# The scores of two heads in the two halves of the array's rows, and the mask as further products

## The chip, the cores and the metric

The kernel runs on one core of a Trainium2 chip. The metric is the device time of one execution in microseconds. Three runs of the kernel before gave 319.25, 321.22 and 318.66 us, a median of 319.25 us. The engines are written as in the profile: PE is TensorE's products and PEld its weight loads, DVE is VectorE, ACT is ScalarE, POOL is GpSimd, SP is SyncE.

## What is computed

A block-sparse attention is followed by a feed-forward block with a residual. For each query row an upper bound of its scores is worked out for each chunk of 32 keys from the chunk's least and greatest key values; the six chunks with the largest bounds are kept, and the softmax runs over the kept keys that are not in the future. Inputs are float32, with 4 batches, 8 heads, 768 rows and a head dimension of 64; the feed-forward block has a width of 512 and a hidden width of 2048.

```python
k_min = np.min(k_chunks, axis=3)
k_max = np.max(k_chunks, axis=3)
ub = np.sum(np.maximum(q[:, :, :, None, :] * k_min[:, :, None, :, :], q[:, :, :, None, :] * k_max[:, :, None, :, :]), axis=-1)
ub = np.where(causal, ub, -1000000000.0)
top_chunks = np.argsort(ub, axis=-1)[..., -top_k:]
scores = scale * np.matmul(q, k.transpose(0, 1, 3, 2))
mask = sel & (pos[:, None] >= pos[None, :])
scores = np.where(mask, scores, -1000000000.0)
attn = softmax(scores)
attn_out = np.matmul(attn, v)
...
xn = (x - mu) / np.sqrt(var + 1e-06) * g_ln
ch = np.maximum(xn @ w_ch1, 0.0) @ w_ch2
return x + ch
```

## The kernel before

The 768 rows are 6 tiles of 128 (`NT`), taken in two halves of 3 tiles (`NR`, `TR`). The 32 heads are taken as 16 pairs (`g`, of which `HP` = 4 belong to one batch). A pair's q and k are loaded half by half with the two heads side by side (`load_qk`, L189, on SP's queue) and turned by TensorE, so that rows 0 to 63 of a turned tile hold head 0 and rows 64 to 127 head 1 (`turn`, L210). v comes through POOL's queue (`load_v`, L198), one transfer a head.

Then, for each pair, or for each half of the first four pairs:

- `k_bound` (L252) takes the chunks' minima and maxima on VectorE; `k_diag` (L274) spreads them over a block layout with `hsel`, in the order of the heads that the mask needs.
- `bounds` (L291) works out the upper bounds by products. In the first four pairs it first runs six products on TensorE whose results nobody reads (`IDLE`).
- `select` (L322) finds the sixth largest bound (`max`) and writes a mask `mn` with 1 where a chunk isn't chosen; `mask_t` (L341) turns it on TensorE, and `mask_ring` (L347) copies it from there.
- `scores` (L385) forms the scores of one half of the rows in bins of at most four blocks of 128 by 128 and applies the exponential with ScalarE (L403). The first half has 2 bins, the second 4. `diag` (L408) cuts the diagonal blocks on POOL, `values` (L415) multiplies by v, `normalise` (L428) divides by the sum, `pair_stats` (L453) takes the statistics for the layer norm.

The scores and the mask are one product of 128 rows. For each head there are tiles of four ring places: `KA` and `QA` for head 0, `KB` and `QB` for head 1. In `KA` rows 0 to 63 are head 0's keys and rows 64 to 127 a constant pattern `RT`, which says for each key in which chunk it lies (times a large negative number). In `QA` rows 0 to 63 are the queries and rows 64 to 127 the turned mask. `KB` and `QB` have the halves the other way round. So a product sums the score and the mask's penalty in one pass:

```python
nc.tensor.matmul(
    sc[:, hh, o:o + w * P], ks[:, t * P:(t + 1) * P], qs[:, s * P:(s + w) * P],
    start=True, stop=True,
)
```

The rings are filled in three ways. In the first four pairs ScalarE copies each 64-row half straight from the turned tile (L227, L228, L266, L267). In the other twelve it copies all 128 rows to `qh` and `kh` (L237, L270), and SP moves the halves into the rings by four transfers for the keys (L271, L272, twice) and two for the queries (`q_ring`, L248). VectorE copies the two halves of the mask (L350, L351), sets the constant rows (`ring_rows`, L107) and clears places without a mask (`ring_init`, L103).

For each batch and half, `stats`, `centre` and `x_t` (L479) make the normalised, turned rows, `mlp1` (L491) and `mlp2` (L504) run the feed-forward block, `rstd` (L477, POOL) and L516 finish a tile, and SP stores it (L521). w1 and w2 are loaded through POOL's queue in four transfers each; a small copy from a pair's `kc` ahead of each one holds it back (`w1_load`, L158, and `w2_load`, L163).

The order of work comes from two lists. `begin` is a hand-made order for the first four pairs and the first rows of batch 0, kept on each compute engine by dependencies (the last lines of the function). All else has a due time (`at(t, ...)`) and is issued sorted by it; a pair takes one unit of time, and the feed-forward work of the last batch is spread between the pairs of the next. The feed-forward work of batch 3 comes last.

Of the kernel before, what the change touches and what calls it, by code (L numbers as in the profile page):

```python
# [19 lines left out]
def kernel(  # L20
# [23 lines left out]
    VW = 72  # L44
    HP = H // 2
    NG = B * HP
# [14 lines left out]
    ring = ctx.enter_context(tc.tile_pool(name="ring", bufs=1))  # L61
# [29 lines left out]
    NK = 4  # L91
    QA = [ring.tile([P, S], F16, name=f"QA{i}", tag=f"QA{i}") for i in range(NK)]
    QB = [ring.tile([P, S], F16, name=f"QB{i}", tag=f"QB{i}") for i in range(NK)]
    KA = [ring.tile([P, S], F16, name=f"KA{i}", tag=f"KA{i}") for i in range(NK)]
    KB = [ring.tile([P, S], F16, name=f"KB{i}", tag=f"KB{i}") for i in range(NK)]

    NB = 3
    BD = [ring.tile([P, 2, 2, NCH], F32, name=f"BD{i}", tag=f"BD{i}") for i in range(NB)]
    BH = [ring.tile([P, 2, 2, 2, NCH], F16, name=f"BH{i}", tag=f"BH{i}") for i in range(NB)]
    NM = 3  # L100
    MN = [ring.tile([P, NT - 1, P], F16, name=f"MN{i}", tag=f"MN{i}") for i in range(NM)]

    def ring_init(i):  # L103
        nc.vector.memset(QA[i][64:P, 0:P], 0.0)
        nc.vector.memset(QB[i][0:64, 0:P], 0.0)

    def ring_rows(i):  # L107
        nc.vector.tensor_copy(KA[i][64:P, :], RT[0:64, :])
        nc.vector.tensor_copy(KB[i][0:64, :], RT[0:64, :])

    def consts_first():
# [10 lines left out]
        )  # L122
        nc.gpsimd.memset(causb, 0.0)
# [6 lines left out]
        nc.vector.memset(hsel[0:64, 0, 1:2], -KS)  # L130
        nc.vector.memset(hsel[64:P, 0, 0:1], -KS)
        nc.vector.memset(hsel[0:64, 1:3, 1:2], KS)
        nc.vector.memset(hsel[64:P, 1:3, 0:1], KS)
# [64 lines left out]
    def load_v(g, i=None):  # L198
        b, hp = divmod(g, HP)
        a, z = (0, NT) if i is None else parts(g)[i]  # L200
        if not i:
            st[g]["va"] = vap.tile([P, 2, NT, VW], F16, name="va", tag="va")
            nc.gpsimd.memset(st[g]["va"][:, :, :, D:D + 1], 1.0)
        for hh in range(2):
            nc.gpsimd.dma_start(  # L205
                st[g]["va"][:, hh, a:z, 0:D],
                v[b, 2 * hp + hh, a * P:z * P].rearrange("(t p) d -> p t d", p=P),
            )
# [10 lines left out]
    def q_copy(g, i):  # L219
        pst = st[g]["qn", i]  # L220
        if g < HP:
            u = P if i == 0 else 0
            for e, (nm, sign) in enumerate((("q32", -1.0), ("r32", 1.0))):
                st[g][nm] = prp.tile([P, TR * P], F32, name=nm, tag=nm)
                nc.scalar.activation(st[g][nm][:, u:], pst[:, u:], ACTF.Relu, scale=sign)
            c = cols(g, i)
            nc.scalar.activation(QA[g % NK][0:64, c], pst[0:64, :], ACTF.Copy, scale=QS)  # L227
            nc.scalar.activation(QB[g % NK][64:P, c], pst[64:P, :], ACTF.Copy, scale=QS)  # L228
            return
        if i == 0:  # L230
            for nm in ("q", "r"):
                t2 = prp.tile([P, 2, S], F16, name=nm + "2", tag=nm + "32")
                st[g][nm + "h"], st[g][nm + "l"] = t2[:, 0], t2[:, 1]
        qh, ql = st[g]["qh"], st[g]["ql"]
        a, z = parts(g)[i]
        u = slice(max(a, 1) * P, z * P)
        nc.scalar.activation(qh[:, cols(g, i)], pst, ACTF.Copy, scale=QS)  # L237
# [9 lines left out]

    def q_ring(g):  # L248
        nc.sync.dma_start(QA[g % NK][0:64, :], st[g]["qh"][0:64, :])
        nc.sync.dma_start(QB[g % NK][64:P, :], st[g]["qh"][64:P, :])  # L250

# [133 lines left out]
    def scores(g, r, i):  # L385
# [6 lines left out]
        for hh in range(2):  # L392
            qs = (QA if hh == 0 else QB)[g % NK]
            ks = (KA if hh == 0 else KB)[g % NK]
            o = 0
            for t, s, w in bins[i]:
                nc.tensor.matmul(  # L397
                    sc[:, hh, o:o + w * P], ks[:, t * P:(t + 1) * P], qs[:, s * P:(s + w) * P],
                    start=True, stop=True,
                )  # L400
                o += w * P
# [139 lines left out]
    begin = [(warm, 8)] + [(ring_init, i) for i in range(NK)] + [(ring_rows, 0)]  # L541
# [6 lines left out]
    for n in range(-3, U):  # L548
# [26 lines left out]
        if n < 0:  # L575
            begin += [(ring_rows, n + 4)]
# [17 lines left out]
    for g in range(HP, NG):  # L594
# [13 lines left out]
        at(T - 1.4, q_ring, g)  # L608
# [89 lines left out]
```

## Time and profile before

| what | value |
|---|---|
| median of three runs | 319.25 us |
| profiled execution, its own time | 319.25 us |
| its span, first to last instruction | 317.5 us |
| granted TensorE clock, mean | 0.993 |
| score products, L397 (two lines of the page: 224 each) | 448 products, 34.8 + 34.1 us shown |
| w1 products, L498, and w2 products, L510 | 95.8 us and 96.6 us shown |
| exponential, L403 | 96 instructions, 85.8 us |
| load of v, L205 | 40 issues, 833 ns each on POOL |
| transfers into the rings | KA, KB 24 each of 48 KB; QA, QB 12 each of 96 KB |

A product's length in such a table is from its start to its modelled end, and products overlap, so the sum of lengths is more than the time they take of the engine; the distance from start to start is what one costs. A name like `KA` stands for all its places. The share of an engine is an average over the span, and a stretch of the span can have another bound.

### The profile page before, as it was taken

The page shows a single profiled execution, that of the slowest core. Times are in us where ns is not written, and L with a number is a line of the kernel's source. Part 1 is how long each engine was busy: PE and PEld are TensorE (multiplying, and loading weights), DVE is VectorE, ACT ScalarE, POOL GpSimd, SP SyncE. Part 2 cuts the span into 40 slices and gives each one's busy share as a digit, 9 for nine tenths or more (in the row PEclk, how much of TensorE's full clock was granted, in tenths as well). Part 3 has the DMA queues.
Part 4 walks back from the last instruction along what each step waited for, and adds up shares of the span by engine and source line. Part 5 has one row for each costly group of instructions (what it writes and reads, how often), then busy time and mean ns, then how long its engine had stood idle before and what let it go on. Part 6 is the DMA issues. An engine that isn't in the chain of part 4 may idle for free.

```text
span 317.5 us, 7210 instructions
## 1 busy us (share of the span) xinstructions
PE 293.0 (92%) x2756; PEld 196.3 (62%) x2756; DVE 190.4 (60%) x646; ACT 183.7 (58%) x274; POOL 98.4 (31%) x174
## 2 busy tenths in 40 slices
PE   7868699977999999889999998999999999999994
PEld 4867376654678767566676756766666565555541
DVE  7877734548977688988856677756653453000021
ACT  4998386544497765567857575566555653333210
POOL 9527705139535434533432122212120211000000
PEclk9999799999999999999999999999999999999999
DMA  7989994999957489464964021020200000100011
GB/s 130 210 152 210 206 188 78 196 171 129 219 138 106 106 133 154 138 77 116 148 81 104 35 77 41 12 72 25 62 35 35 33 33 2 66 35 33 33 69 67
DMA packets 90419, 31.42 MB, mean 99 GB/s; under 512 B 78608, under 2 KB 87312, under 8 KB 90384
## 3 DMA queue, kind: packets, MB, share of 16 engines
q1 hardware_dynamic: 60416, 23.61, 31.7%
q0 software_dynamic: 29440, 7.34, 24.3%
q8 instruction: 22, 0.36, 0.5%
q14 instruction: 13, 0.11, 0.1%
q10 hardware_dynamic: 528, 0.00, 0.1%
HBM read 27.27 MB, written 6.29 MB: 106 GB/s over the span
## 4 chain that ended last, share of the span: by engine, by line
PE 65%; DVE 13%; issue 6%; DMA 5%; POOL 4%; ACT 4%; SPq 2%; ACTq 0%; POOLq 0%
PE yp L510 24%; PE mm L498 19%; PE mm L397 7%; PE sm L423 5%; PE tr L214 4%; DMA w2b<-in_moe_w_ch_dram 3%; PE ub L317 3%; DVE bst L457 2%; PE trh L483 2%; POOL va L205 2%; DVE x L433 2%; SPq L194 2%; DVE xc L468 2%; DMA qn<-in_q_dram 1%; ACT pt L403 1%
## 5 line engine op out<-in xcount | busy, mean ns | idle before, releaser
L403 ACT ACTIVATE pt<-mm 128x1024 f16<-128x1024 f32 x96 | 85.8, 917 | 38.8 <-PE mm L397 38.1
L510 PE MATMUL yp<-w2b,hT 128*128 128x512 f16 x384 | 96.6, 379 | 1.9 <-DMA w2b<-in_moe_w_ch_dram 1.9
L498 PE MATMUL mm<-xT,w1b 128*128 128x384 f16 x512 | 95.8, 329 | 1.4 <-ACT pt L403 1.2
L502 ACT ACTIVATE hT<-mm 128x768 f16<-128x768 f32 x64 | 51.9, 811 | 57.0 <-PE mm L498 56.8
L498 PEld LDWEIGHTS <-w1b 128*128 128x128 f16 x512 | 49.4, 99 | 33.5 <-issue 3.6
L410 POOL TENSOR_SCALAR_AFFINE_SELECT pt<-pt 128x768 f16<-128x768 f16 x32 | 29.5, 923 | 96.6 <-ACT pt L403 96.6
L510 PEld LDWEIGHTS <-hT 128*128 128x128 f16 x384 | 36.9, 98 | 34.6 <-DMA w2b<-in_moe_w_ch_dram 2.3
L516 DVE SCALAR_TENSOR_TENSOR ot<-yp,rstd,x 128x512 f32<-128x512 f32 x24 | 17.9, 745 | 55.9 <-PE yp L510 54.0
L397 PE MATMUL mm<-QA,KA 128*128 128x128 f16 (+2 forms) x224 | 34.8, 245 | 1.0 <-ACT hT L502 0.9
L397 PE MATMUL mm<-QB,KB 128*128 128x128 f16 (+2 forms) x224 | 34.1, 246 | 0.1
L205 POOL DMA_DIRECT2D va<-in_v_dram x40 | 33.0, 833 | 1.0 <-issue 0.5
L423 PEld LDWEIGHTS <-pt 128*128 128x128 f16 x672 | 25.4, 98 | 6.2 <-issue 1.1
L423 PE MATMUL sm<-va,pt 128*128 128x65 f16 x672 | 27.0, 193 | 1.2 <-ACT QB L228 1.0
L432 DVE RECIPROCAL rden<-sm 128x6 f32<-128x6 f32 x32 | 6.2, 193 | 31.8 <-PE sm L423 31.8
L397 PEld LDWEIGHTS <-KA 128*128 128x128 f16 x224 | 17.9, 98 | 7.4 <-issue 1.0
L457 DVE BATCH_NORM_STATS2 bst<-x 128x6 f32<-128x128 f32 x96 | 21.7, 280 | 0.8
L397 PEld LDWEIGHTS <-KB 128*128 128x128 f16 x224 | 17.9, 98 | 4.2 <-issue 1.3
L238 DVE SCALAR_TENSOR_TENSOR q<-tr,q 128x256 f16<-128x256 f32 (+1 forms) x24 | 11.6, 485 | 14.5 <-ACT q L237 14.2
L259 DVE TENSOR_REDUCE kc<-tr 128x12 f32<-128x384 f32 x32 | 17.5, 546 | 4.5 <-PE tr L214 4.5
L433 DVE TENSOR_TENSOR x<-sm,rden 128x384 f32<-128x384 f32 x32 | 17.8, 556 | 1.0
L483 PE MATMUL trh<-ident_h,xc 128*128 128x128 f16 x96 | 10.5, 224 | 7.7 <-DVE xc L468 6.5
L214 PE MATMUL tr<-ident_f,qn 128*128 128x128 f32 x96 | 16.2, 278 | 1.5 <-DMA qn<-in_q_dram 1.5
(83 smaller groups left out, 349.9 us busy)
## 6 DMA issues: line engine op xcount, KB each, us to landing
kn<-in_k_dram SPq DMA_DIRECT2D x64, 96.0 KB, 3.0
qn<-in_q_dram SPq DMA_DIRECT2D x64, 96.0 KB, 3.5
out_dram<-ot SPq DMA_DIRECT2D x24, 256.0 KB, 2.1
va<-in_v_dram POOLq DMA_DIRECT2D x24, 96.0 KB, 4.4
w1b<-in_moe_w_ch_dram POOLq DMA_DIRECT2D x4, 512.0 KB, 8.1
w2b<-in_moe_w_ch_dram POOLq DMA_DIRECT2D x4, 512.0 KB, 8.9
KA<-kh SPq DMA_DIRECT2D x24, 48.0 KB, 2.0
KB<-kh SPq DMA_DIRECT2D x24, 48.0 KB, 2.0
```

Of the source, the lines that this page charges most:

```text
L205: nc.gpsimd.dma_start(st[g]["va"][:, hh, a:z, 0:D], v[b, 2 * hp + hh, a * P:z * P].rearrange("(t p) d -> p t d", p=P),)
L214: nc.tensor.transpose(pst[:, t * P:(t + 1) * P], src[:, t], ident_f)
L397: nc.tensor.matmul(sc[:, hh, o:o + w * P], ks[:, t * P:(t + 1) * P], qs[:, s * P:(s + w) * P], start=True, stop=True,)
L403: nc.scalar.activation(pt[:, n0:n1].rearrange("p n h x -> p h n x"), sc[:, :, 0:o].rearrange("p h (n x) -> p h n x", x=P), ACTF.Exp, scale ...
L410: nc.gpsimd.affine_select(out=dv, in_=dv, compare_op=ALU.is_ge, fill=0.0, base=0, pattern=[[0, 2 * TR], [1, P]], channel_multiplier=-1,)
L423: nc.tensor.matmul(pv[:, hh, s2, :], pt[:, where[t, s], hh, :], va[:, hh, t, 0:D + 1], start=(t == 0), stop=(t == s),)
L433: nc.vector.tensor_tensor(xh(b, r)[:, :, 2 * hp:2 * hp + 2, :].rearrange("p s h d -> p h s d"), pv[:, :, :, 0:D], rden.to_broadcast([P, 2, ...
L457: nc.vector.bn_stats(h["st"][:, i, hp], xh(b, r)[:, i, 2 * hp:2 * hp + 2].rearrange("p h d -> p (h d)"),)
L498: nc.tensor.matmul(hp_[:, i, 0:TR * P], w1b[:, kt, (m + i) * P:(m + i + 1) * P], h["xT"][:, kt], start=(kt == 0), stop=(kt == KT1 - 1),)
L502: nc.scalar.activation(h["hT"][:, m:m + 2], hp_[:, :, 0:TR * P], ACTF.Relu, scale=HS)
L510: nc.tensor.matmul(yp, h["hT"][:, kt, i * P:(i + 1) * P], w2b[:, kt, :], start=(kt == 0), stop=(kt == KT2 - 1),)
L516: nc.vector.scalar_tensor_tensor(ot, yp, h["rstd"][:, i:i + 1], xh(b, r)[:, i].rearrange("p h d -> p (h d)"), op0=ALU.mult, op1=ALU.add,)
```

## The change

It lets each head's scores be a product of 64 rows: head 0 from rows 0 to 63 of `kh` and `qh`, head 1 from rows 64 to 127 of the same tiles. The mask is added by further products of 64 rows, of `RT` and the turned mask `mt`, into the same sums. `RT` has its pattern in both halves now. For each bin the products of the scores come first and then those of the mask, and the heads alternate. Block (0,0) needs no mask product. A bin of one head is one sum: its first product starts it, its last one ends it.

The rings with their copies and transfers go (`ring_init`, `ring_rows`, `q_ring`, L271, L272). `qh`, `kh` and `mt` come from a pool with five buffers each; BD, BH and MN move to the constants' pool. In the first four pairs a half's keys or queries are copied by one instruction of 128 rows, and the mask everywhere by one. `hsel` has the heads in their own order. For the pairs from 4 on v is loaded by one transfer a pair. Twelve products whose results nobody reads (`idle`, 128 by 512) come before the first `x_t`.

```diff
+    NK = 5
...
-    ring = ctx.enter_context(tc.tile_pool(name="ring", bufs=1))
+    ring = ctx.enter_context(tc.tile_pool(name="ring", bufs=NK))
...
+        nc.vector.tensor_copy(RT[64:P, :], RT[0:64, :])
...
     def load_v(g, i=None):
         b, hp = divmod(g, HP)
-        a, z = (0, NT) if i is None else parts(g)[i]
+        if i is None:
+            va = st[g]["va"] = vap.tile([P, 2, NT, VW], F16, name="va", tag="va")
+            nc.gpsimd.memset(va[:, :, :, D:D + 1], 1.0)
+            nc.gpsimd.dma_start(
+                va[:, :, :, 0:D].rearrange("p h t d -> p (h t) d"),
+                v[b, 2 * hp:2 * hp + 2].rearrange("h (t p) d -> p (h t) d", p=P),
+            )
+            return
+        a, z = parts(g)[i]
...
-            c = cols(g, i)
-            nc.scalar.activation(QA[g % NK][0:64, c], pst[0:64, :], ACTF.Copy, scale=QS)
-            nc.scalar.activation(QB[g % NK][64:P, c], pst[64:P, :], ACTF.Copy, scale=QS)
+        if i == 0:
+            st[g]["qh"] = ring.tile([P, S], F16, name="qh", tag="qh")
+        qh = st[g]["qh"]
+        nc.scalar.activation(qh[:, cols(g, i)], pst, ACTF.Copy, scale=QS)
+        if g < HP:
             return
...
-    def q_ring(g):
-        nc.sync.dma_start(QA[g % NK][0:64, :], st[g]["qh"][0:64, :])
-        nc.sync.dma_start(QB[g % NK][64:P, :], st[g]["qh"][64:P, :])
...
     def k_copy(g, i):
         pst = st[g]["kn", i]
-        c = cols(g, i)
-        if g < HP:
-            nc.scalar.copy(KA[g % NK][0:64, c], pst[0:64, :])
-            nc.scalar.copy(KB[g % NK][64:P, c], pst[64:P, :])
-            return
-        kh = smp.tile([P, TR * P], F16, name="kh", tag="kh")
-        nc.scalar.copy(kh, pst)
-        nc.sync.dma_start(KA[g % NK][0:64, c], kh[0:64, :])
-        nc.sync.dma_start(KB[g % NK][64:P, c], kh[64:P, :])
+        if i == 0:
+            st[g]["kh"] = ring.tile([P, S], F16, name="kh", tag="kh")
+        nc.scalar.copy(st[g]["kh"][:, cols(g, i)], pst)
...
-        nc.vector.tensor_copy(QA[g % NK][64:P, a * P:z * P], pm[64:P, 0:(z - a) * P])
-        nc.vector.tensor_copy(QB[g % NK][0:64, a * P:z * P], pm[0:64, 0:(z - a) * P])
+        if i is None or i == 0:
+            st[g]["mt"] = ring.tile([P, S], F16, name="mt", tag="mt")
+        nc.vector.tensor_copy(st[g]["mt"][:, a * P:z * P], pm[:, 0:(z - a) * P])
...
+    def idle(n, w=512):
+        junk = ps_t.tile([P, 512], F32, name="idle", tag="one")
+        for _ in range(n):
+            nc.tensor.matmul(junk[:, 0:w], MN[0][:, 0, :], MN[0].rearrange("p s c -> p (s c)")[:, 0:w], start=True, stop=True)
...
         sc = ps_m.tile([P, 2, 512], F32, name="mm", tag="mm")
-        for hh in range(2):
-            qs = (QA if hh == 0 else QB)[g % NK]
-            ks = (KA if hh == 0 else KB)[g % NK]
-            o = 0
-            for t, s, w in bins[i]:
+        o, todo = 0, []
+        for t, s, w in bins[i]:
+            todo.append((st[g]["kh"], st[g]["qh"], t, s, w, o))
+            o += w * P
+        for _, _, t, s, w, f in todo[:]:
+            c = int(s == 0)
+            if w > c:
+                todo.append((RT, st[g]["mt"], t, s + c, w - c, f + c * P))
+        for n, (ks, qs, t, s, w, f) in enumerate(todo):
+            for hh in range(2):
+                row = slice(64 * hh, 64 * hh + 64)
                 nc.tensor.matmul(
-                    sc[:, hh, o:o + w * P], ks[:, t * P:(t + 1) * P], qs[:, s * P:(s + w) * P],
-                    start=True, stop=True,
+                    sc[:, hh, f:f + w * P], ks[row, t * P:(t + 1) * P], qs[row, s * P:(s + w) * P],
+                    start=(n == 0), stop=(n == len(todo) - 1),
                 )
-                o += w * P
...
-    begin = [(warm, 8)] + [(ring_init, i) for i in range(NK)] + [(ring_rows, 0)]
+    begin = [(warm, 8)]
...
-            begin += [(x_t, 0, 0, kt) for kt in range(KT1)]
+            begin += [(idle, 12)] + [(x_t, 0, 0, kt) for kt in range(KT1)]
...
-        if n < 0:
-            begin += [(ring_rows, n + 4)]
...
-        at(T - 1.4, q_ring, g)
```

More of the change, by code (lines that the diff above doesn't have):

```diff
@@ L90 @@
     mhalf = const.tile([P, TR], F32, name="mhalf", tag="mhalf")
[L91 to L95, printed above, removed]
     NB = 3
-    BD = [ring.tile([P, 2, 2, NCH], F32, name=f"BD{i}", tag=f"BD{i}") for i in range(NB)]
-    BH = [ring.tile([P, 2, 2, 2, NCH], F16, name=f"BH{i}", tag=f"BH{i}") for i in range(NB)]
+    BD = [const.tile([P, 2, 2, NCH], F32, name=f"BD{i}", tag=f"BD{i}") for i in range(NB)]
+    BH = [const.tile([P, 2, 2, 2, NCH], F16, name=f"BH{i}", tag=f"BH{i}") for i in range(NB)]
     NM = 3
[L101 to L109, printed above, removed]
+    MN = [const.tile([P, NT - 1, P], F16, name=f"MN{i}", tag=f"MN{i}") for i in range(NM)]
     def consts_first():
@@ L129, in consts_first @@
         nc.scalar.activation(tiny, hsel[0:1, 0, 0:1], ACTF.Exp)
[L130 to L133, printed above, removed]
+        nc.vector.memset(hsel[0:64, 0, 0:1], -KS)
+        nc.vector.memset(hsel[64:P, 0, 1:2], -KS)
+        nc.vector.memset(hsel[0:64, 1:3, 0:1], KS)
+        nc.vector.memset(hsel[64:P, 1:3, 1:2], KS)
         for i in range(NM):
@@ L225, in q_copy @@
                 nc.scalar.activation(st[g][nm][:, u:], pst[:, u:], ACTF.Relu, scale=sign)
-            c = cols(g, i)
-            nc.scalar.activation(QA[g % NK][0:64, c], pst[0:64, :], ACTF.Copy, scale=QS)
-            nc.scalar.activation(QB[g % NK][64:P, c], pst[64:P, :], ACTF.Copy, scale=QS)
+        if i == 0:
[3 more added lines that the diff above has]
+        if g < HP:
             return
         if i == 0:
[L231 to L234, printed above, removed]
+            t3 = prp.tile([P, 3, S], F16, name="q3", tag="q3")
+            st[g]["ql"], st[g]["rh"], st[g]["rl"] = t3[:, 0], t3[:, 1], t3[:, 2]
+        ql = st[g]["ql"]
         a, z = parts(g)[i]
         u = slice(max(a, 1) * P, z * P)
-        nc.scalar.activation(qh[:, cols(g, i)], pst, ACTF.Copy, scale=QS)
         nc.vector.scalar_tensor_tensor(
```

## The prediction

> **What bounds the kernel now.** I read the page's first part and the chain of waits first, to see which engine sets the end.
>
> ```profile
> PE 293.0 (92%) x2756; PEld 196.3 (62%) x2756; DVE 190.4 (60%) x646; ACT 183.7 (58%) x274; POOL 98.4 (31%) x174
> ...
> PE 65%; DVE 13%; issue 6%; DMA 5%; POOL 4%; ACT 4%; SPq 2%; ACTq 0%; POOLq 0%
> ```
>
> TensorE is busy 92% of the span and makes up 65% of the chain. But 92% is an average, so next I asked for the busy time by stages.
>
> ```profile
> 13.00:17.40 4.40, 3.42 (x47) 3.35 (x46) 3.13 (x10) 4.31 (x10) 0.85 (x1) 1.00 1.34 213
> ...
> 36.80:40.20 3.40, 3.40 (x17) 2.11 (x15) 1.36 (x9) 0.53 (x2) 2.49 (x5) 0.57 1.26 190
> 40.20:45.00 4.80, 4.33 (x36) 3.29 (x35) 1.90 (x5) 4.74 (x10) 0.00 (x0) 1.00 1.35 196
> ...
> 75.00:80.00 5.00, 3.08 (x30) 1.89 (x27) 4.51 (x14) 0.87 (x2) 5.00 (x10) 1.00 1.88 165
> ...
> 125.00:137.00 12.00, 10.05 (x112) 6.42 (x112) 11.10 (x33) 7.14 (x11) 6.30 (x10) 1.00 0.65 128
> ...
> 198.00:250.00 52.00, 52.00 (x509) 34.79 (x510) 29.65 (x100) 30.74 (x41) 8.64 (x15) 1.00 0.13 37
> ```
>
> After the stretch and its length the columns are PE, PEld, DVE, ACT, POOL (busy us and count), the granted clock and the DMA share. The reader sees three regimes. In 13 to 17.4 and 40.2 to 45 ScalarE is full (4.31 of 4.40, 4.74 of 4.80). In 75 to 80 and 125 to 137 VectorE is nearly full and TensorE has holes. In 198 to 250 TensorE has none at all. The idle time of TensorE between 40 and 262 us is small, and its waits say whose it is:
>
> ```profile
> PE trh L483 <- DVE xc L468: 4.0, 4, 1.9
> PE yp L510 <- DMA w2b<-in_moe_w_ch_dram: 1.9, 1, 1.9
> PE mm L498 <- ACT pt L403: 1.2, 3, 0.5
> PE mm L397 <- ACT hT L502: 0.9, 2, 0.5
> ```
>
> So from 40 us on any added TensorE time goes almost whole into the end, and relief of the other engines can win only these few microseconds. Last, the price of products, from the timeline of TensorE (start, length, group):
>
> ```profile
> 118.40 1.07 PE L423 MATMUL sm<-va,pt 128*128 128x65 f16 x30
> 119.31 0.39 PE L397 MATMUL mm<-QA,KA 128*128 128x128 f16 x4
> 119.54 0.39 PE L397 MATMUL mm<-QB,KB 128*128 128x128 f16 x4
> 119.76 0.25 PE L317 MATMUL ub<-BH,q 128*128 128x96 f16 x2
> ```
>
> A product is shown 219 ns long, but eight start within 0.45 us: 56 ns per 128 columns. The 30 products of 65 columns start within 0.91 us, 30 ns each, and each of them loads new weights. The loads are hidden.
>
> **The score products.** Per pair and head there are 21 blocks of 128 columns in 14 products, so the kernel has 448 products and 16 x 42 = 672 blocks, at about 55 ns some 37 us. Afterwards each head has the same 14 products with 64 rows, and 13 more with 64 rows that add the mask (20 blocks, as block (0,0) has none): 864 products in 432 twos, one of each head. If the two of a two run at the same time in the two halves of the array, the time is that of 16 x 41 = 656 blocks: 16 x 55 ns = **0.9 us less**. If they run one after the other, 1312 blocks are 640 more than now, +35 us. No row of this trace has two products at once. The narrowest step the trace shows for load and product is 30 ns, so a two needs up to 60 ns where 128 columns need 56. 17 of the 27 twos of a pair are that narrow: 272 x 4 ns = **1.1 us more**, the value I take, because the weight path of the 30 ns row is the nearest thing to what a two asks for; 0 and +35 us stay as ends. By the span model of "TensorE: Matmul & The Clock Gate" (Part 3, packing small matmuls) a further row tile would add about 4 ns: an estimate of 432 x 4 ns = 1.7 us in place of the 1.1 us, which no run here shows.
>
> **The changes of the tile's shape.** All products of before are 128*128. In the instruction order of the changed kernel the 864 form 93 runs between 128-row products: 186 changes. The nearest row is a change of operand type: at 13.48 the last f16 score product (256 columns, 105 ns) is followed at 13.59 by an f32 transpose, with no gap beyond its columns. That bounds a change from below at **0**; a gain is excluded since nothing is removed there. From above it is the whole overlap lost, 219 - 56 = 163 ns, 186 x 163 = 30 us. I take 0 by the nearest row, and keep the upper end. "TensorEngine Tiling (Array Packing)", Key Properties, speaks against the change: it says that switching the tiling mode drains the engine. It names no time; a drain as long as the overlap would make the sum some 30 us worse, the row makes it nothing.
>
> **ScalarE at the front.** In the first eight half-pairs four copies of 64 rows (L227, L228, L266, L267; 473 to 486 ns) become two of 128 rows, and a copy's time follows its columns: 477 to 494 ns for 128x384 at L270 and L237. That is 16 x 0.48 = 7.7 us of ScalarE. What is on the path:
>
> ```profile
> 16.50 0.48 ACT L228 ACTIVATE QB<-tr 64x384 f16<-64x384 f32 x1
> ...
> 17.04 0.52 PE L423 MATMUL sm<-va,pt 128*128 128x65 f16 x12 [0.98 <-ACT QB L228]
> ```
>
> The first values product waits 0.98 us for L228 behind a full ScalarE; with one copy less ahead of it, 0.9 us go. From 17.4 to 31.7 the loop is another: values, L433, the statistics (0.68), maxima, mask transposes, bounds, values again, about 5 us, none of it removed: 0. In 40.2 to 45 ScalarE is full again and TensorE waits for it (0.47 us at L397, as much before L498): 0.9 us.
>
> **The twelve idle products.** They stand before the x_t of the first half, where TensorE now idles 1.89 + 0.43 + 0.16 us and then runs at clock 0.50 from about 36.8 to 39.7. Eight w1 products there take 320 ns each instead of 162: 1.3 us. The idle products (12 x 216 = 2.6 us, the spacing of 512 columns in L510) end at about 35.2, before the third xc at 35.6, which is waited for anyway; they cost 0.1. I take 1.2 us.
>
> These three, **3.0 us**, must pass the w2 transfer that TensorE waits for until 66.7. Its issue stands on POOL behind the diag of 50.56, which waits for an exp at 49.46, so it moves with the front. If the transfers do not come earlier, these 3.0 us are lost: that end is 0.
>
> **VectorE.** The two mask copies of 64 rows (495 and 480 ns) become one of 128: 0.48 us for each of the 12 later pairs, 0.28 for the first ones, and ring_rows and ring_init (4.1 us before 13 us, beside transfers that are waited for) go against one RT copy of about 0.45. It counts only where TensorE waits for VectorE: 75 to 80, 125 to 137, 137 to 147, 184 to 198, four stretches, of which one copy lies before the xc in each: at most 4 x 0.48 = 1.9, I take **1.5 us**; lower end 0.
>
> **Queues.** The 72 transfers from SBUF to SBUF leave SP, where kn and qn loads stood behind the waits of L271 (34.9 us in all). TensorE waits for no load after 11 us, so 0. One copy on ScalarE waited 3.7 us for such a transfer near 76, beside the xc wait of 1.92 that set the pace there: nothing beyond the term above. POOL issues 12 loads of v fewer: 12 x 0.83 us, in stretches where it waits for ScalarE (96.6 us), so 0; if one issue of twelve tiles took twice as long, it would be 0 too. The new ring of five for kh, qh and mt is waited for by none, as the reader of a buffer is five pairs back.
>
> **The sum**, from the profiled run (319.25 us, of which 317.5 is the span, and also the median of the three): -0.9 + 1.1 + 0 - 3.0 - 1.5 = -4.3, so **315.0 us**. It would be no different by more than 1% between 316.1 and 322.4.
>
> **Rivals.**
> - *The change of shape empties the array* (slower). Place: each of about 176 changes behind the front. For it: nothing covers TensorE in 198 to 250. Against it: the change of type is free. At half of its bound, 82 ns, it costs 14 us: **329 us**. It decides from 4.3 us / 186 = 23 ns on, and costs over 1% from about 41 ns (7.4 us). Chance 0.25.
> - *The halves do not run together*: 315 + 35 = **350 us**. PEld of the 128-row products is hidden now, which says nothing of halves. Chance 0.10.
> - *The relief stays off the path*: the w2 transfers land when they do now, and VectorE's copies lie in waits. What is left is -0.9 + 1.1 and the 1.0 us or so of single waits: **318.5 us**. For it: DMA is over 1.2 in most of 36 to 66 us. Chance 0.18; 0.02 more for small changes of shape that just cancel the gain.
> - *More goes*: the waits listed above vanish as well, about 5 us: **310 us**. Chance 0.05.
>
> My own case has 0.40, with a range of its own of 311 to 316. So faster has 0.45, same 0.20, slower 0.35. The range goes from 309 to 333: it leaves out the serial case and the upper end of the first rival, 0.16, and 0.03 below.
>
> **What will show it.** Right: a run of 7 twos (4 of the scores, 3 of the mask, all of 128 columns) passes in about 0.42 us and the next group starts without a gap; the first values product starts near 16.1; the clock is 1.00 in 36 to 40; the wait for w2 ends near 63.7; the stretch of 52 products at the end is unchanged. Wrong: gaps of tens of ns at both ends of each run of 64-row products, or steps of 56 ns for each single one, either of which would show in a longer 198 to 250; or an exposed wait for w2 that has grown by what the front won.

## The result and the profile after

The changed kernel takes 330.64 us, the median of four runs (330.31 to 334.62); the kernel before took 319.91 us beside it (four runs, 318.66 to 321.22). The ratio is 1.036, with an interval of 1.027 to 1.046: 3.6% slower. The profiled execution took 330.31 us, of which 328.1 are its span, against 319.25 and 317.5 before; so the two traces are 11.06 us apart.

First the page of the changed kernel: busy time by engine, the chain of waits by engine and by line, and from the list of the costliest groups the score products, the mask products and the weight loads in front of the former (after the bar: idle time just before them, and what ended most of it). "Issue" is time in which an engine waited for nothing that the profile can name.

```profile
PE 309.9 (94%) x3184; PEld 191.0 (58%) x3184; DVE 177.6 (54%) x611; ACT 177.2 (54%) x258; POOL 90.4 (28%) x162
...
PE 75%; DVE 16%; ACT 3%; SPq 2%; issue 1%; DMA 1%; POOL 1%; POOLq 0%
PE yp L508 24%; PE mm L496 22%; PE mm L396 9%; PE sm L421 5%; PE tr L211 4%; PE ub L304 3%; DVE bst L455 3%; DVE x L431 2%; PE ub L294 2%; PE trh L481 2%; SPq L183 2%; PE trh L332 1%; DVE xc L466 1%; DVE q L235 1%; ACT hT L500 1%
...
L396 PE MATMUL mm<-qh,kh 64*128 64x128 f16 (+2 forms) x448 | 37.0, 246 | 2.4 <-ACT pt L401 1.3
L396 PE MATMUL mm<-mt,RT 64*128 64x128 f16 (+2 forms) x416 | 33.9, 245 | 0.0
...
L396 PEld LDWEIGHTS <-kh 64*128 64x128 f16 x448 | 15.6, 94 | 22.5 <-issue 20.0
```

All that the change was to relieve is relieved: VectorE has 177.6 us instead of 190.4, ScalarE 177.2 instead of 183.7, POOL 90.4 instead of 98.4. DMA has gone from 5% of the chain to 1%. TensorE has gone from 65% to 75%. The last line is the one to stop at. The weight loads stood idle for 20.0 us ahead of the score products with the releaser "issue": they waited for no semaphore, no transfer, no engine that the profile names. The kernel before had 1.0 and 1.3 us of that at the same place, for head 0 and head 1:

```profile
L397 PEld LDWEIGHTS <-KA 128*128 128x128 f16 x224 | 17.9, 98 | 7.4 <-issue 1.0
...
L397 PEld LDWEIGHTS <-KB 128*128 128x128 f16 x224 | 17.9, 98 | 4.2 <-issue 1.3
```

Then the stretches, with the columns of the prediction's table (PE, PEld, DVE, ACT, POOL, clock, DMA share, GB/s). They are fixed in time, so the later ones hold somewhat other work than before.

```profile
13.00:17.40 4.40, 4.40 (x63) 3.90 (x59) 2.92 (x10) 3.66 (x7) 0.85 (x1) 1.00 1.36 205
36.80:40.20 3.40, 3.40 (x33) 2.41 (x31) 1.66 (x5) 3.21 (x7) 2.00 (x3) 1.00 1.44 216
40.20:45.00 4.80, 4.80 (x60) 3.21 (x61) 1.14 (x4) 2.38 (x3) 0.00 (x0) 1.00 1.38 207
75.00:80.00 5.00, 5.00 (x43) 2.64 (x42) 4.90 (x12) 1.53 (x3) 2.81 (x5) 1.00 1.99 182
125.00:137.00 12.00, 9.87 (x119) 5.62 (x116) 10.59 (x33) 6.05 (x9) 5.75 (x10) 1.00 0.49 83
198.00:250.00 52.00, 51.17 (x557) 30.17 (x555) 29.66 (x102) 29.40 (x40) 9.19 (x15) 1.00 0.06 22
```

At the front TensorE is full where it had holes, ScalarE is no longer full, and the clock is 1.00 in 36.8 to 40.2 where it was 0.57. In 198 to 250, where TensorE had no idle time before, it is still shown busy for 51.17 of 52 us. That number hides the loss: a product of 128 columns is shown some 220 ns long whatever its distance from the next, so a gap of 100 ns between starts doesn't appear as idle time of PE. It must be read from the starts. The waits of TensorE for other engines, at least, have shrunk, and the w2 transfer is no longer among them:

```profile
PE trh L481 <- DVE xc L466: 3.6, 5, 1.3
PE trh L332 <- DVE MN L323: 2.9, 4, 1.0
...
PE mm L396 <- ACT pt L401: 1.3, 3, 0.6
```

Now the starts, from the timeline of TensorE (start, length, group) around one bin of a later pair. The bin has one score product and four mask products for each head, 128 columns each:

```profile
206.98 1.03 PE L508 MATMUL yp<-w2b,hT 128*128 128x512 f16 x4
207.94 0.23 PE L396 MATMUL mm<-qh,kh 64*128 64x128 f16 x2
208.01 0.39 PE L396 MATMUL mm<-mt,RT 64*128 64x128 f16 x8
208.32 0.66 PE L496 MATMUL mm<-xT,w1b 128*128 128x384 f16 x3
```

and the weight loads of the same time:

```profile
206.87 0.64 PEld L508 LDWEIGHTS <-hT 128*128 128x128 f16 x4
207.94 0.10 PEld L396 LDWEIGHTS <-kh 64*128 64x128 f16 x2 [0.42 <-issue]
207.95 0.27 PEld L396 LDWEIGHTS <-RT 64*128 64x128 f16 x8
208.32 0.44 PEld L496 LDWEIGHTS <-w1b 128*128 128x128 f16 x4
```

Two things are read here. Ten products of 128 columns pass between 207.94 and 208.32, in 0.38 us; one after the other they would need 10 x 56 ns = 0.56. So the two products of a two (one of each head) do run together: in the trace most start 3 to 4 ns apart (377 of the 421 that can be told apart; 32 start 16 to 20 ns apart), and twos follow each other every 56 ns. And 0.38 is 0.10 more than 5 x 56 ns. The last two starts at 208.18 and the next w1 product, of 128 rows, 148 ns later instead of 56. At the other end the last w2 product starts at 207.63 and the first two 312 ns later, where w2 products of 512 columns are 216 ns apart. The loads show the same gap: none of the new shape starts before 207.94, when the first product of that shape starts too, 0.10 us behind the columns of the last w2 product (0.42 us of "issue").

Over the whole trace a change between f16 products of the two shapes has a median of 98 to 99 ns beyond the columns, in both directions (97 to an f32 transpose); products of one shape have 2 to 3 ns. The second two of a 64-row run starts another 10 ns later than that (median of 74 runs). There are 186 changes: 186 x 97 ns = **18.0 us**. How the difference grows along the run (start of the same product before and after, and the difference less 97 ns for each change up to then):

| product | before | after | difference | less the changes |
|---|---|---|---|---|
| first values product | 17.04 | 15.47 | -1.57 | -1.76 |
| w1, first | 36.86 | 35.31 | -1.55 | |
| w1, ninth | 40.24 | 37.34 | -2.90 | |
| w2, 13th | 66.73 | 63.13 | -3.59 | -6.11 |
| values, 169th | 89.73 | 85.65 | -4.08 | -7.96 |
| w2, 97th | 163.24 | 165.28 | +2.04 | -8.24 |
| w2, 241st (all scores done) | 263.81 | 274.85 | +11.04 | -7.00 |
| w2, last | 312.54 | 323.59 | +11.04 | -7.00 |

The kernel is 4 us ahead at 86 us, loses that and 11 us more by 275 us at the pace of the changes, and nothing after the last bin. By this count the rest has won 7.0 us without the changes. The last column takes the full 97 ns for each change, also where TensorE would have waited anyway, so its rows near the front are too large; the first experiment has the leads without any change.

### The profile page after: what moved, and what is told of

Same layout as the page of the kernel before. It is cut to its first block, busy times and chain, and to the rows that moved or that the text cites. A ratio compares the mean times of both kernels' runs of the same rounds, so it can differ in the third digit from the quotient of the medians.

```text
span 328.1 us, 7854 instructions
## 1 busy us (share of the span) xinstructions
PE 309.9 (94%) x3184; PEld 191.0 (58%) x3184; DVE 177.6 (54%) x611; ACT 177.2 (54%) x258; POOL 90.4 (28%) x162
## 4 chain that ended last, share of the span: by engine, by line
PE 75%; DVE 16%; ACT 3%; SPq 2%; issue 1%; DMA 1%; POOL 1%; POOLq 0%
PE yp L508 24%; PE mm L496 22%; PE mm L396 9%; PE sm L421 5%; PE tr L211 4%; PE ub L304 3%; DVE bst L455 3%; DVE x L431 2%; PE ub L294 2%; PE trh L481 2%; SPq L183 2%; PE trh L332 1%; DVE xc L466 1%; DVE q L235 1%; ACT hT L500 1%
## 5 line engine op out<-in xcount | busy, mean ns | idle before, releaser
L401 ACT ACTIVATE pt<-mm 128x1024 f16<-128x1024 f32 x96 | 86.8, 918 | 48.9 <-PE mm L396 48.5
L496 PE MATMUL mm<-xT,w1b 128*128 128x384 f16 x512 | 94.1, 326 | 0.8 <-ACT pt L401 0.7
L408 POOL TENSOR_SCALAR_AFFINE_SELECT pt<-pt 128x768 f16<-128x768 f16 x32 | 27.7, 865 | 113.1 <-ACT pt L401 113.1
L508 PEld LDWEIGHTS <-hT 128*128 128x128 f16 x384 | 35.2, 98 | 37.3 <-issue 6.1
L396 PE MATMUL mm<-qh,kh 64*128 64x128 f16 (+2 forms) x448 | 37.0, 246 | 2.4 <-ACT pt L401 1.3
L396 PE MATMUL mm<-mt,RT 64*128 64x128 f16 (+2 forms) x416 | 33.9, 245 | 0.0
L396 PEld LDWEIGHTS <-kh 64*128 64x128 f16 x448 | 15.6, 94 | 22.5 <-issue 20.0
L235 DVE SCALAR_TENSOR_TENSOR q<-tr,qh 128x256 f16<-128x256 f32 (+1 forms) x24 | 11.7, 489 | 18.8 <-ACT qh L226 18.6
L259 ACT CAST kh<-tr 128x384 f16<-128x384 f32 x32 | 15.5, 484 | 10.5 <-DVE kc L253 8.9
L252 DVE TENSOR_REDUCE kc<-tr 128x12 f32<-128x384 f32 x32 | 17.6, 549 | 6.5 <-PE tr L211 6.5
L396 PEld LDWEIGHTS <-RT 64*128 64x128 f16 x416 | 17.2, 94 | 2.0
L431 DVE TENSOR_TENSOR x<-sm,rden 128x384 f32<-128x384 f32 x32 | 17.8, 556 | 0.9
L253 DVE TENSOR_REDUCE kc<-tr 128x12 f32<-128x384 f32 x32 | 17.6, 549 | 0.0
```

The source lines that it names most:

```text
L252: nc.vector.tensor_reduce(kc[:, 0, n], view, axis=AX.X, op=ALU.min)
L396: nc.tensor.matmul(sc[:, hh, f:f + w * P], ks[row, t * P:(t + 1) * P], qs[row, s * P:(s + w) * P], start=(n == 0), stop=(n == len(todo) - 1),)
L401: nc.scalar.activation(pt[:, n0:n1].rearrange("p n h x -> p h n x"), sc[:, :, 0:o].rearrange("p h (n x) -> p h n x", x=P), ACTF.Exp, scale ...
L408: nc.gpsimd.affine_select(out=dv, in_=dv, compare_op=ALU.is_ge, fill=0.0, base=0, pattern=[[0, 2 * TR], [1, P]], channel_multiplier=-1,)
L431: nc.vector.tensor_tensor(xh(b, r)[:, :, 2 * hp:2 * hp + 2, :].rearrange("p s h d -> p h s d"), pv[:, :, :, 0:D], rden.to_broadcast([P, 2, ...
L496: nc.tensor.matmul(hp_[:, i, 0:TR * P], w1b[:, kt, (m + i) * P:(m + i + 1) * P], h["xT"][:, kt], start=(kt == 0), stop=(kt == KT1 - 1),)
```

## The experiments

Two theories stood at the start. *Shape*: each change of the tile's height costs TensorE some 97 ns, so the loss goes by the number of changes. *Work*: the narrower products themselves are dearer, by their number (864 instead of 448), their loads or their sums in PSUM. The first four kernels tell these apart; the kernel before took 320.29 us beside them (seven runs).

**rows128: the same work in products of 128 rows.** The number of product blocks is that of before, with bank 0 taking `kh` by `qh` and bank 1 `kh` by `mt`; no product has 64 rows.

```diff
-        for n, (ks, qs, t, s, w, f) in enumerate(todo):
-            for hh in range(2):
-                row = slice(64 * hh, 64 * hh + 64)
+        for t, s, w in bins[i]:
+            c = int(s == 0)
+            each = [(0, qh, s, w, o)]
+            each += [(1, qh, s, 1, o)] if c else []
+            each += [(1, mt, s + c, w - c, o + c * P)] if w > c else []
+            for hh, qs, s, w2, f in each:
...
-                    sc[:, hh, f:f + w * P], ks[row, t * P:(t + 1) * P], qs[row, s * P:(s + w) * P],
+                    sc[:, hh, f:f + w2 * P], kh[:, t * P:(t + 1) * P], qs[:, s * P:(s + w2) * P],
```

> The changed kernel with its score products in 128 rows: the same stationary and moving tiles, of all 128 rows, the scores' products into the first head's bank and products of kh with mt into the second's, 672 blocks and no product of 64 rows. It leaves out the heads' separation and the penalty, so its values are not the reference's. Theory 'shape' (a change between products of 64 and 128 rows costs about 97 ns): 186 changes go, 18.0 us, and 16 blocks more cost 0.9: 313 us. Rival 'work' (more products and loads, or the new order and waits, cost the time, and a change of shape is free): about 330 us.

Measured: 313.65 us (312.86 to 314.78), 0.981 of the kernel before (0.976 to 0.987). That is 17.0 us below the changed kernel; 186 changes less the 16 blocks that the changed kernel saves come to 18.0 - 0.9 = 17.1. On its page the loads of the score products no longer wait for "issue" (10.2 us idle, 1.5 of it so named):

```profile
L401 PE MATMUL mm<-qh,kh 128*128 128x128 f16 (+2 forms) x240 | 42.0, 244 | 0.6 <-ACT hT L506 0.5
L401 PE MATMUL mm<-mt,kh 128*128 128x128 f16 (+2 forms) x208 | 41.7, 248 | 0.0
...
L401 PEld LDWEIGHTS <-kh 128*128 128x128 f16 x448 | 32.7, 98 | 10.2 <-issue 1.5
```

Its starts give the leads over the kernel before that the changed kernel would have without its changes of shape (and without the 16 blocks saved):

| product | before | rows128 | lead |
|---|---|---|---|
| first values product | 17.04 | 15.48 | 1.6 |
| w1, ninth | 40.24 | 37.22 | 3.0 |
| w2, 13th | 66.73 | 61.82 | 4.9 |
| values, 169th | 89.73 | 84.21 | 5.5 |
| w2, last | 312.54 | 306.28 | 6.3 |

At the 169th values product the changed kernel is only 1.4 us behind rows128 with 40 changes (3.9 us at 97 ns): much of the front's changes passes in waits. Behind it, over the other 146 changes, it loses 15.9 us more, where 97 ns each make 14.2. So the agreement of 17.0 with 17.1 is partly luck.

So everything in the change but the shape is worth a gain, and *work* falls as far as all but the count of products goes. rows128 has fewer products too (448 instead of 864), so in the next pair the kernel with more changes is the one with fewer products.

**zero64 and zero128: the same added columns, with and without two more changes a bin.** Between the scores and the mask of a bin a product of a tile of zeros is added to the sums, which leaves them as they are: in zero64 as a two of 64 rows, in zero128 as one of 128 rows, 128 columns in both.

```diff
+                if n == len(bins[i]) - 1:
+                    nc.tensor.matmul(sc[:, hh, 0:P], zero[row, :], zero[row, :], start=False, stop=False)
```

```diff
+            if n == len(bins[i]) - 1:
+                nc.tensor.matmul(sc[:, 0, 0:P], zero, zero, start=False, stop=False)
```

> The changed kernel with a two of 64-row products of a zero tile (128 columns) between the scores' and the mask's products of each of the 96 bins; they add zero. 'shape': 96 x 56 ns = 5.4 us and 8 changes fewer in the order, so about 335 us. 'work': the same or more, 336 us.

> As zero64, but one product of 128 rows of the zero tile at that place, so that each bin has two more changes of shape (362 in the order instead of 178 in zero64). 'shape': 5.4 us as in zero64 and 176 x 97 ns = 17.1 us above the changed kernel, so about 353 us, 17 to 18 above zero64. 'work': one product in place of two, no slower than zero64, about 335 us.

Measured: 336.19 us (336.02 to 336.29) and 345.99 us (345.77 to 346.20). The timeline of zero128 around a bin of four blocks:

```profile
210.04 0.40 PE L398 MATMUL mm<-qh,kh 64*128 64x128 f16 x8
210.37 0.23 PE L403 MATMUL mm<-zero 128*128 128x128 f16 x1
210.53 0.34 PE L398 MATMUL mm<-mt,RT 64*128 64x128 f16 x6
210.80 0.50 PE L500 MATMUL mm<-xT,w1b 128*128 128x384 f16 x2
```

Four twos of scores take 4 x 56 = 0.22 us and 0.33 pass until the zero product; its 128 columns take 0.06 and 0.16 pass until the mask; three twos take 0.17 and 0.27 pass until w1. Each of the three changes costs 0.10 us, and with fewer products (one in place of two) zero128 is the slower kernel by 9.8 us. That is *shape*, and *work* expected the reverse order. The size was missed, though: by their instruction orders the kernels have 178 and 362 changes, and 184 x 97 ns = 17.8 us were due where 9.8 came. To see where the rest is, I split the distances between starts in all the traces: changes at 97 ns each, and what else exceeds the columns by more than 30 ns, which is waits of TensorE for others (and, in the kernel before, products at half clock).

| kernel | changes | at 97 ns, us | other gaps, us |
|---|---|---|---|
| before | 0 | 0 | 31.2 |
| rows128 | 0 | 0 | 22.4 |
| after | 186 | 18.0 | 20.3 |
| zero64 | 178 | 17.3 | 21.1 |
| zero128 | 362 | 35.1 | 12.9 |
| bins_in_twos | 118 | 11.4 | 34.0 |

From zero64 to zero128 the changes cost 17.8 us more and the other gaps shrink by 8.2: where TensorE waited for VectorE or ScalarE, the changes pass in the time of the waits. The lists of waits say the same: those for xc, MN, pt and hT, which VectorE and ScalarE write, fall from 10.0 to 2.0 us. From rows128 to after only 2.1 us were hidden in that way, which is why nearly the full price showed there.

**bins_in_twos: fewer changes by another order.** The bins of the later pairs come due two at a time, so that a run of 64-row products covers two bins.

```diff
-                t += 0.14
+                t += 0.28 * (i % 2)
```

> The changed kernel with the due times of a later pair's bins set so that two bins stand together: 118 changes of shape instead of 186, all products kept. 'shape': 68 x 97 ns = 6.6 us less, 324 us, or up to 3 us more where two bins wait for two free buffers. 'work': 330 us or more.

Measured: 336.56 us (336.19 to 336.90), 5.9 us slower than the changed kernel; a miss for *shape*, which expected a gain. By the time alone it is where *work* put it (330 us or more). The table has another reason. The 68 changes saved are worth 6.6 us, and they were saved; but the other gaps grew by 13.7. The waits of TensorE name where:

```profile
PE mm L496 <- ACT pt L401: 8.9, 20, 1.1
...
PE ub L304 <- POOL BH L276: 1.9, 3, 0.8
```

Scores and w1 products share the `mm` buffers in PSUM. Two bins in a row fill them, and the next w1 product waits for ScalarE's exponential (L401), 8.9 us in 20 waits, where the changed kernel had 0.7 us of them: 8.2 of the 13.7 us. The spacing of the bins hides the exponential, and the spacing is what makes 186 changes.

**The parts without a change of shape.** The next kernels ask where the 7.0 us come from. The kernel before took 320.65 us beside these (23 runs).

before_idle and before_v_one are the kernel before with one part each, after_no_idle is the changed kernel less its idle products:

```diff
-            begin += [(x_t, 0, 0, kt) for kt in range(KT1)]
+            begin += [(idle, 12)] + [(x_t, 0, 0, kt) for kt in range(KT1)]
```

> The kernel before with the twelve idle products alone. By the prediction's term: 1.2 us less, 319.1 us, clock 1.00 in 36 to 40 us. If TensorE's slow clock there is covered by another wait: 320.3 us or more.

> The changed kernel without the twelve idle products. By the prediction's term 1.2 us more, 331.8 us, with a clock under 1 in 34 to 40 us. If they cost more than they bring: under 330 us.

before_v_one has the change's `load_v`:

```diff
-        a, z = (0, NT) if i is None else parts(g)[i]
+        if i is None:
+            va = st[g]["va"] = vap.tile([P, 2, NT, VW], F16, name="va", tag="va")
+            nc.gpsimd.memset(va[:, :, :, D:D + 1], 1.0)
+            nc.gpsimd.dma_start(
+                va[:, :, :, 0:D].rearrange("p h t d -> p (h t) d"),
+                v[b, 2 * hp:2 * hp + 2].rearrange("h (t p) d -> p (h t) d", p=P),
+            )
+            return
+        a, z = parts(g)[i]
```

> The kernel before with one transfer of v a pair from pair 4 on, alone. By the prediction's term 0: 320.3 us within 1. If POOL's issues hold back the diagonals and BH: 1 to 3 us less.

Measured: before_idle 317.71 us (ratio 0.990, 0.987 to 0.994), so 2.9 us less where 1.2 were expected; before_v_one 318.46 us (0.996, 0.993 to 1.000); after_no_idle 331.77 us (ratio 1.034, 1.030 to 1.039). The last one's median is 1.1 us above the changed kernel's 330.64, but its ratio is not above the 1.036 of that, so the times alone leave it open; in the traces the ninth w1 product starts at 38.53 instead of 37.34 us and the last w2 product at 324.53 instead of 323.59, 0.9 to 1.2 us later. How the idle products work is seen in the stretches (the number behind the last bracket is the granted clock). The kernel before, ahead of the stretch at clock 0.57:

```profile
31.70:36.80 5.10, 2.28 (x30) 1.59 (x27) 4.29 (x13) 2.78 (x4) 3.29 (x5) 0.95 1.31 212
```

and before_idle in both:

```profile
31.70:36.80 5.10, 4.61 (x36) 2.59 (x34) 4.34 (x14) 2.99 (x4) 3.47 (x5) 1.00 1.27 216
36.80:40.20 3.40, 3.40 (x27) 2.37 (x26) 2.32 (x11) 2.13 (x5) 2.31 (x3) 1.00 1.34 186
```

TensorE is busy for 4.61 instead of 2.28 of 5.10 us, the difference with work that nobody reads, the clock stays at 1.00, and the next 3.4 us hold 27 products in place of 17. The last w2 product starts 1.9 us earlier than before (310.64 against 312.54); the two traces are of executions of 317.35 and 319.25 us, which are closer to each other than the medians.

**front_only: the relief at the front alone.** The kernel before, with scores and mask of the first four pairs as in the change (32 changes of shape), the rings set up for the later pairs only, with the idle products and one transfer of v. The core of the edit, besides the one-instruction copies:

```diff
+            for n, (ks, qs, t, s, w, f) in enumerate(todo):
+                for hh in range(2):
+                    row = slice(64 * hh, 64 * hh + 64)
...
-        for hh in range(2):
+        for hh in range(0 if g < HP else 2):
...
-    begin = [(warm, 8)] + [(ring_init, i) for i in range(NK)] + [(ring_rows, 0)]
+    begin = [(warm, 8)]
...
+        if n > HP:
+            begin += [(ring_rows, n - HP - 1), (ring_init, n - HP - 1)]
```

> The kernel before with the change in the first four pairs alone: there the scores are 64-row products (216 of them, 32 changes of shape in the order), with one copy each of keys, queries and mask; from pair 4 on the rings, as before. The constant rows of the rings are set later, the twelve idle products and one transfer of v a pair are in. 'shape': 32 x 97 ns = 3.1 us for the changes, of which the ten before 32 us lie in waits; against it the gain that the changed kernel's rows show by its 64th w1 product, 7.9 us without the price of the changes: 320.3 - 7.9 + 3.1, about 315 to 316 us, faster than both. 'relief is small' (the gain came from the later pairs' queues and copies): 319 to 322 us.

Measured: 320.93 us (12 runs, 319.63 to 322.06; ratio 1.002, 0.999 to 1.005), the time that was expected if the relief at the front is small. But the front is relieved: the 13th w2 product starts at 63.45 us against 66.73 before, with 0.2 us of wait for w2 left of 1.9, so the front has won 3.3 us. At the 169th values product nothing is left (90.28 against 89.73). In between, ScalarE waits for the transfer that empties a `kh` buffer into the ring (the kernel before has 3.7 us of this wait):

```profile
ACT kh L282 <- DMA KB<-kh: 4.3, 1, 4.3
```

So the next kernel, front_kh5, gave `kh` five buffers in front_only, and idle_kh5 did the same to before_idle:

```diff
-        kh = smp.tile([P, TR * P], F16, name="kh", tag="kh")
+        kh = smp.tile([P, TR * P], F16, name="kh", tag="kh", bufs=5)
```

> The kernel front_only with five buffers in place of two for kh in the later pairs, so that ScalarE's copy of a pair's keys need not wait for the transfers of the keys before it. If that wait (4.3 us at 78 us in front_only) gives back what the front won, the wait goes, the 3.3 us that the front is ahead at 64 us last to the end, and the time is 317 to 318 us. If the rings' transfers and the load beside them are late in themselves, ScalarE's wait only moves to a load or the products of the scores wait for KB, and the time stays at 320 to 321 us.

> The kernel before_idle with five buffers in place of two for kh. In before_idle ScalarE's copy of the keys waited 3.7 us for a load of qn and not for KB<-kh, so the deeper kh should change nothing by itself: 317.7 us, within 0.5. If kh's two buffers hold the order of SP's queue up all along, it is 1 to 2 us less, 316 to 317.

Measured, with the kernel before at 320.66 us (29 runs): 320.44 us (ratio 1.001, 0.998 to 1.004) and 318.06 us (0.995, 0.992 to 0.998). The wait for KB<-kh is gone from ScalarE, which waits for VectorE's `kc` instead (4.2 us at the longest), and the time is the same, so that wait took nothing; idle_kh5 lies within 0.5 us of before_idle's 317.71, as was expected if the buffers change nothing. TensorE's longest wait in front_kh5 is for another engine:

```profile
PE trh L522 <- DVE xc L507: 5.9, 5, 3.9
```

The longest of the five took 3.9 us and ended at 79 us (front_only has the same one). VectorE in front of it (start, length, group):

```profile
73.56 0.20 DVE L471 RECIPROCAL rden<-sm 128x6 f32<-128x6 f32 x1 [1.34 <-PE sm L462]
...
75.62 0.35 DVE L108 COPY KA<-RT 64x768 f16<-64x768 f16 x1
75.99 0.35 DVE L109 COPY KB<-RT 64x768 f16<-64x768 f16 x1
76.39 0.11 DVE L104 MEMSET QA<- 64x64 uint32 x1
76.56 0.11 DVE L105 MEMSET QB<- 64x64 uint32 x1
...
78.47 1.35 DVE L507 TENSOR_SCALAR xc<-x,mv 128x512 f16<-128x512 f32 x3
```

The set-up of the rings, which the kernel before does ahead of 13 us, stands here in front of the xc. front_rows_act puts the copies of L108 and L109 on ScalarE:

```diff
-        nc.vector.tensor_copy(KA[i][64:P, :], RT[0:64, :])
-        nc.vector.tensor_copy(KB[i][0:64, :], RT[0:64, :])
+        nc.scalar.copy(KA[i][64:P, :], RT[0:64, :])
+        nc.scalar.copy(KB[i][0:64, :], RT[0:64, :])
```

> The kernel front_kh5 with the copies of the constant rows into KA and KB on ScalarE in place of VectorE. In front_kh5 four of them (0.35 us each) and four small clears stand on VectorE between 67.2 and 76.6 us, ahead of the xc at 78.47 us that TensorE waits 3.9 us for. If they are what takes the front's gain back, that xc comes 1 to 2 us earlier and the time falls by as much, to 318.5 to 319.5 us. If xc is late because of what VectorE itself waits for (values at 73.6 us, the loads), the wait stays above 3 us and the time at 320 to 321 us.

Measured: 319.38 us (12 runs, 317.57 to 320.93; ratio 0.996, 0.994 to 0.999; the kernel before 320.80). The xc:

```profile
77.85 1.36 DVE L507 TENSOR_SCALAR xc<-x,mv 128x512 f16<-128x512 f32 x3
```

It comes 0.62 us earlier and the median is 1.1 us lower than that of front_kh5, though the intervals of the two ratios just touch; 3.1 us of wait are left. So the ring set-up is a part of the wait. What else makes the xc late (VectorE itself waits for the values until 73.56) is not settled.

The wait has a second price, which stands in the stretches of front_only:

```profile
75.00:78.00 3.00, 0.00 (x0) 0.00 (x0) 2.85 (x12) 0.00 (x0) 0.36 (x1) 1.00 2.28 176
78.00:81.50 3.50, 2.75 (x15) 1.65 (x16) 3.04 (x8) 1.06 (x2) 2.89 (x5) 0.51 1.87 180
```

Behind the hole of TensorE the clock is granted by half for 3.4 us, from 78.1 to 81.5 (79.7 to 83.1 in front_kh5, 79.2 to 82.6 in front_rows_act); the kernel before has 1.00 there. From the 13th w2 to the 169th values product front_only takes 26.8 us and the kernel before 23.0. By the distances between starts, about 1.9 of these 3.8 us are longer waits, 1.4 are products at half clock and 0.6 the six changes of shape. So the idle products removed the half clock at 36 to 40, and in these kernels another one stands behind the wait for the xc. The changed kernel, whose rings are gone altogether, waits at most 1.3 us for an xc, has clock 1.00 there and keeps its lead over that stretch.

**idle_v_one: the two parts that won alone, together, on the kernel before.**

> The kernel before with the two small parts of the change that cost no change of shape: the twelve idle products and one transfer of v a pair. If the two gains (2.9 and 1.2 us against the kernel before) add up, 316.5 us. If both fill the same hole, 317.7 us.

Measured: 317.15 us (12 runs, 316.75 to 318.87), 0.993 of the kernel before (0.990 to 0.997). That lies between the two expected times, and before_idle's 317.71 is within the spread, so a gain of the one transfer beyond what the idle products give is not shown. With rows128 aside, which leaves part of the computation out, these two are the fastest kernels of all the runs, 13 us below the changed one.

## Why the prediction was wrong

It forecast 315.0 us and faster; 330.64 came, which lies in its range, at the first rival's time (329) and on the other side of no change.

**The step that failed** is "The changes of the tile's shape": "I take 0 by the nearest row, and keep the upper end." The row was a change of operand type from an f16 product to an f32 transpose, and it is free (a median of 3 ns, as between f16 products). A change of shape has nothing to do with it: it measured 97 ns, beyond the middle of the bounds of 0 and 163 ns, and 186 x 97 ns = 18.0 us took the place of the 0 (rows128 against the changed kernel: 17.0 us). The page "TensorEngine Tiling (Array Packing)" of the Trainium skill, Key Properties, which the prediction had weighed against the row, says that switching the mode drains the engine. The traces agree: medians of 97 to 99 ns beyond the columns each way, with the loads of the new shape idle on "issue". With a row that shows another thing against a rule that names this very thing, the choice should have been by the middle of the bounds (82 ns, the rival's 329 us), not by the row. The rival's threshold of 23 ns was there to warn: a seventh of the upper bound was enough to turn the sign.

**The rest of the sum** was -4.3, and the trace has -7.0 when all changes count in full. rows128 has neither the blocks saved nor the twos, so of the sum -3.0 and -1.5 hold for it, 314.8 us; it came to 313.65, and its trace ends 6.3 us ahead in place of 4.5. By terms:

- *Fewer blocks, halves together* (-0.9): right by the spacing, two products in 56 ns; no run measures the 0.9 by itself. The serial rival (350) falls.
- *Two loads for a two* (+1.1): mis-sized. Twos of 128 columns follow each other at 56 ns with a median excess of 3 ns, as 128-row products do, so this is 0. The 4 ns a tile of the skill's page "TensorE: Matmul & The Clock Gate" (Part 3) are there as the distance of the two starts in most twos, and not as added time from two to two.
- *ScalarE at the front* (0.9 and 0.9): too small in both places. Between the ninth w1 and the 13th w2 product, where the second 0.9 belongs, rows128 wins 1.9. The first values product comes 1.57 earlier, at 15.47 us instead of the expected 16.1:

```profile
15.47 0.53 PE L421 MATMUL sm<-va,pt 128*128 128x65 f16 x12
```

- *The twelve idle products* (1.2): right in place, and near in size for the changed kernel: from the first to the ninth w1 product the lead grows by 1.35, and without them the trace is 0.9 to 1.2 us longer. On the kernel before they win more: 1.9 by the traces, 2.9 by the medians (1.9 to 4.3 by the ratio's interval).
- *The lead must pass the w2 transfer* ("the wait for w2 ends near 63.7"): right. The product stands at 63.13 and waits no longer, and the rival in which the relief stays off the path (318.5) falls.
- *VectorE* (1.5): right in size as far as rows128 shows it. Behind the 13th w2 product its lead grows by 1.4 us, from 4.9 to 6.3; that VectorE's copies alone make this up is not shown. front_rows_act adds that it matters whether the rings' set-up is gone or only moved, by about 1 us of the median.
- *Queues* (0): before_v_one came out at 0.996, with an interval that nearly reaches 1, and idle_v_one shows nothing clear beyond before_idle. Nothing here contradicts the 0.

Of what was to show it, "gaps of tens of ns at both ends of each run of 64-row products" came, at 97 to 99 ns; "the clock is 1.00 in 36 to 40" came too, and "the stretch of 52 products at the end is unchanged" held to 0.01 us.

## What to carry to other kernels

Count the changes of tile shape in the order of instructions before splitting the array's rows: at 97 ns each, a run of a few narrow products between full ones pays 0.2 us, while the split of a full product in two halves gave only 2% of the blocks back. Grouping the narrow products is not free either when their spacing is what hides the engine that reads them. Where the cheapest value of an unknown price comes from a row that shows a different operation, and a small part of its upper bound would turn the sign, the forecast is the middle and not the cheap end.

## What the hardware showed beyond that

- A change between products of 64 and of 128 rows costs 97 to 99 ns beyond the columns (medians of the changed kernel), the same in both directions; behind the lone 128-row products of zero128 the change to 64 rows has a median of 108. The step from an f16 or bf16 product to an f32 one at one shape has medians of 3 to 6 ns.
- A profile's busy time doesn't show it. In 198 to 250 PE is shown busy for 51.17 of 52 us, and 42 changes, 4.1 us, lie in that stretch; the place on the page that does is the idle time of the weight loads ahead of the score products put down to "issue" (20.0 us against 1.0 and 1.3).
- Added TensorE time is not additive where TensorE waits for others: 17.8 us of changes between zero64 and zero128 cost 9.8.
- Twelve products that nobody reads, in holes of TensorE of some 2.5 us together, lift the granted clock of the 3.4 us after them from 0.57 to 1.00, and the kernel before gets 1.9 to 4.3 us faster.
- A wait of 3.9 us in front_only was followed by 3.4 us at half clock, which took 1.4 us more. The front's gain of 3.3 us went into both, and into the changes of shape. A lone wait of 1.9 us near 79 us in the kernel before was not followed by a lower clock.
